# An FFT convolution with phase mixing: the inverse's pieces placed among the spectrum pieces, without idle matmuls

## The chip, the cores and the metric

The kernel runs on one core of one Trainium2 chip. The metric is the device time of one execution in microseconds. Before the change it was 2034.54 us, the median of three runs (2033.99 to 2038.23).

## What is computed

Two stages follow one another. The first convolves each of 8 sequences of 5696 tokens and 128 channels with one filter per channel, by a real FFT of twice the length. The second mixes tokens with two dense 5696 x 5696 matrices after a phase rotation, and ends with a small channel matmul.

```
L = 2 * S                                   # B, S, D = 8, 5696, 128
Yf = rfft(x, n=L, axis=1) * rfft(h, n=L, axis=0)[None]
x  = irfft(Yf, n=L, axis=1)[:, :S]
theta = x @ w_theta
y = w_tok_r @ (x * cos(theta)) + w_tok_i @ (x * sin(theta))
u = x + y
out = u + relu(u @ w_ch)
```

The change concerns only the first stage. In the profiled execution it takes the first 340 us or so, and the dense mixing most of the rest.

## The kernel before, in words

The FFT of length 11392 is split as 178 x 64 and done with matmuls against sine tables. The work is cut into eight groups, each two sequences (index `bp`) by half of the channels (`dh`, 64 channels). A group goes through four stages:

- A, `stage_a` (L251): 16 pieces of 4 matmuls (89 rows, 180 columns each). Each piece is copied from PSUM to the tile `a` by ScalarE (L258).
- B, `stage_b` with `f2` (L269): the spectrum in 12 pieces over the 90 frequencies of the first split, eight frequencies to a piece and two in the last, so 32 matmuls (64 rows, 64 columns) in each of eleven pieces and 8 in the last. ScalarE copies each to `xs` (L399, two buffers), and VectorE multiplies it twice with the filter's spectrum into `u_t` and `v_t` (L401).
- C, `stage_c` (L421, L422): 16 pieces of 16 matmuls (128 x 128). Every one reads all frequencies of `u_t` and `v_t`, so C can't begin before the last products of B. Each piece is scaled into the tile `g` (one buffer), mostly by VectorE (L429). ScalarE does some of the pieces with two instructions (L426, L427).
- D, `stage_d` (L444): the inverse in 7 pieces, six of 20 matmuls (90 rows, 89 columns) and one of 8. The first needs all of `g`. ScalarE copies each to `yt` (L447), and behind the last the result is stored to HBM on SP's queue.

All four stages draw their PSUM tiles from one ring of four buffers (`psum()`), in program order: a piece can't start before the piece four places earlier is copied out.

The loop over groups runs two stages of neighbouring groups together. Loop `g` first weaves C of group `g` with A of group `g + 1`, and then B of group `g + 1` with D of group `g`. The function `woven` gives every step of each list a place between two bounds and runs the steps in order of place, so that the order of each engine's work is the program's order here. With its bounds, C and A begin with three A pieces; B and D run as B0 D0 B1 B2 D1 B3 B4 D2 B5 B6 D3 B7 D4 B8 B9 D5 B10 B11 D6. The load of x for group `g + 2` is the last step of the list of A; its 16 DMAs are issued by GpSimd (L138). In the last loop there is no next group, and steps of the phase stage (`phase_step`, L728 and L515 to L551) are woven in instead.

Behind the last spectrum piece, `f2` issues 12 matmuls of 384 columns on tables (L275, `WARM`). They write columns of the piece's own PSUM tile that nobody reads.

Of the kernel before, what the change touches and what calls it, by code (L numbers as in the profile page):

```python
# [23 lines left out]
def kernel(  # L24
# [10 lines left out]
    nc = tc.nc  # L35
    B, S, D = x.shape
    assert D == 128
    P = 128
# [45 lines left out]
    CK = 8  # L84
    HD = D // 2
    EN = N2 // 2 + 1
    WARM = 12
    XP = HD + 4
    assert N1 * N2 == NF and NB * N2 == S and NB % 2 == 1 and K1 <= P
    CHK = [(c0, min(CK, K1 - c0)) for c0 in range(0, K1, CK)]  # L90
    NCK = len(CHK)
# [36 lines left out]
    groups = [(bp, dh) for dh in range(2) for bp in range(B // 2)]  # L128
# [45 lines left out]
    w_t2 = keep.tile([P, K1, 3 * N2], F16, tag="keep", name="w_t2")  # L174
# [83 lines left out]
                nc.scalar.activation(a_out, a_in, AF.Copy)  # L258
        return [lambda q=q: chunk(q) for q in range(0, HD, 4)], st

    def f2(a_st, c, warm=True):

        c0, ck = CHK[c]
        ps = psum()
        for j in range(ck):
            for ri in range(2):
                for e in range(2):
                    rows = slice(64 * e, 64 * e + 64)
                    nc.tensor.matmul(ps[:, e, j * HD:(j + 1) * HD],  # L269
                                     w_t2[rows, slot(e, c0 + j), N2 * (1 - ri):N2 * (3 - ri)],  # L270
                                     a_st["a"][rows, ri * K1 + c0 + j, :],
                                     start=(ri == 0), stop=(ri == 1))
        if c == NCK - 1 and warm:
            for n in range(WARM):
                nc.tensor.matmul(ps[:, n % 2, ck * HD:ck * HD + 384], w_t2[:, 2, :P],  # L275
                                 w_t2[:, 0:2, :].rearrange("p k n -> p (k n)"), start=True, stop=True)
        return ps[:, :, :ck * HD].rearrange("p e (k d) -> p e d k", k=ck)

    def woven(*lists):

        lists = [l if isinstance(l, tuple) else (l, 0.0, 1.0) for l in lists]
        steps = [(w0 + (i + 0.5) / len(l) * (w1 - w0), n, f)
                 for n, (l, w0, w1) in enumerate(lists) for i, f in enumerate(l)]
        for _, _, f in sorted(steps, key=lambda s: s[:2]):
            f()
# [8 lines left out]
    steps, a_h = stage_a(lambda q: h16[:NB].rearrange("p h n d -> p (h n) d")[:, :, q], (4, 6, 8, 10, 12, 14))  # L294
# [28 lines left out]

    def h_chunk(c):
        c0, ck = CHK[c]
        ps = f2(a_h, c, False)
        nc.scalar.activation(h_part(c)[:, 0], ps[:, 0], AF.Copy, scale=16.0 / NF)
        nc.vector.tensor_scalar(h_later[:, HD * c0:HD * (c0 + ck)].rearrange("p (d k) -> p d k", k=ck),
                                ps[:, 1], 16.0 / NF, None, op0=mult)
# [59 lines left out]
        nc.vector.tensor_scalar(sgn[:, :EN], sgn[:, :EN], half, None, op0=mult)  # L389
        nc.vector.tensor_scalar(sgn[:, EN:], sgn[:, EN:], odd, half, op0=mult, op1=mult)  # L390

    def stage_b(a_st, warm, refill):

        def chunk(c):
            c0, ck = CHK[c]
            hv = h_part(c)
            ps = f2(a_st, c, warm)
            xs = fs.tile([P, 2, HD, CK], F16, tag="xs", name="xs")
            nc.scalar.activation(xs[:, :, :, :ck], ps, AF.Copy)  # L399
            for r in range(2):  # L400
                nc.vector.tensor_tensor(  # L401
                    uv[r][:, :, :, c0:c0 + ck], xs[:, :, :, :ck],
                    hv[:, r:r + 1].to_broadcast([P, 2, HD, ck]), op=mult)
            if refill:
                src = hf_hbm[:, HD * c0:HD * (c0 + ck)]
                nc.sync.dma_start(h_flat(c)[:, :HD * ck], src)
                for p0 in (0, 64):
                    nc.sync.dma_start(h_flat(c)[p0:p0 + 64, HD * ck:], src[64 - p0:P - p0])
        return [lambda c=c: chunk(c) for c in range(NCK)]

    def stage_c(st, last):
        sg = sgn[:K1].unsqueeze(2).unsqueeze(1).to_broadcast([K1, 2, N2, 8])

        def chunk(q):
            if q == 0:
                st["g"] = fg.tile([P, 2 * N2, P], F16, tag="g", name="g_")
            ps = psum()
            for i in range(8):
                o = ps[:, i // 4, (i % 4) * P:(i % 4 + 1) * P]
                at = (q + i) * K1  # L420
                nc.tensor.matmul(o, u_t[:, at:at + P], r_u, start=True, stop=False)  # L421
                nc.tensor.matmul(o, v_t[:, at:at + P], r_v, start=False, stop=True)  # L422
            g_out = st["g"][:K1, :, q:q + 8].rearrange("p (r n) q -> p r n q", r=2)
            g_in = ps[:K1].rearrange("p a (q r n) -> p r n (a q)", q=4, r=2)
            if q % 16 == 0 and (last or q >= 64):
                nc.scalar.mul(g_out[:, :, :EN], g_in[:, :, :EN], sgn[:K1, 0:1])  # L426
                nc.scalar.mul(g_out[:, :, EN:], g_in[:, :, EN:], sgn[:K1, EN:EN + 1])  # L427
            else:
                nc.vector.tensor_tensor(g_out, g_in, sg, op=mult)  # L429
        return [lambda q=q: chunk(q) for q in range(0, 2 * HD, 8)]  # L430

    def stage_d(st, bp, dh, then=None):
        def chunk(n0, cn):
            if n0 == 0:
                st["yt"] = fy.tile([P, NB, N2], BF16, tag="yt", name="yt")
            g_, yt = st["g"], st["yt"]
            ps = psum()
            nq = 5 if cn == CN else cn
            for j in range(cn):
                n = n0 + j  # L440
                o = ps[:, j // nq, (j % nq) * NB:(j % nq + 1) * NB]
                for ri in range(2):
                    e_ = e_t[:K1, n, ri, :] if n < EN else e_t[:K1, N2 - n, ri, ::-1]
                    nc.tensor.matmul(o, g_[:K1, ri * N2 + n, :], e_, start=(ri == 0), stop=(ri == 1))  # L444
            y_out = yt[:, :, n0:n0 + cn].rearrange("p m (a q) -> p m a q", q=nq)
            y_in = ps[:, :cn // nq, :nq * NB].rearrange("p a (q m) -> p m a q", q=nq)
            nc.scalar.activation(y_out, y_in, AF.Copy)  # L447
            if n0 + cn == N2:
                if then is not None:
                    then(yt)  # L450
                for e in range(2):
                    t0 = H if then else 0
                    nc.sync.dma_start(
                        yt_hbm[dh * HD:(dh + 1) * HD, 2 * bp + e, t0:],
                        yt[64 * e:64 * e + 64].rearrange("p m n -> p (m n)")[:, t0:])
        return [lambda n0=n0, cn=cn: chunk(n0, cn) for n0, cn in CHN]
# [3 lines left out]
    def front(g, on_dve=()):  # L460
        if g >= len(groups):
            return [], []
        dh = groups[g][1]
        x16 = x16s[g].rearrange("p b n d -> p (b n) d")
        steps, a_st = stage_a(lambda q: x16[:NB, :, q], on_dve)
        return steps, stage_b(a_st, g > 0, dh == 0 and groups[g + 1][1] == 1)

    a0, b0 = front(0, (2, 4, 6, 8, 10, 12, 14))
    BATCH = ((0, 4), (4, 4), (8, 3), (11, 1))
# [11 lines left out]
    for n, f in enumerate(a0):  # L481
# [9 lines left out]
    e_left = [lambda f=f, n=n: f(*E_STEPS[n]) for f, n in (  # L491
        (e_table, 1), (e_index, 5), (e_table, 2), (e_index, 6), (e_table, 3),
        (e_table, 4), (e_table, 5), (e_table, 6))]
# [261 lines left out]
    for g, (bp, dh) in enumerate(groups):  # L755
        st = {}
        last = g + 1 == len(groups)
        if last:
            late_order.enter_context(tc.manual_schedule(engines={mybir.EngineType.Pool}))
        a_, b_ = front(g + 1, () if g else (5, 11))  # L760
        if last:
            for _ in range(3):
                steps0.pop(0)()
        now = [with_load(steps0.pop(0), n < 6) for n in range(9)] if last else []
        c_ = stage_c(st, last)
        if g + 2 < len(groups):
            a_ = a_ + [lambda g=g: load_x(g + 2)]
        woven((c_, 0.06 if a_ else 0.0, 1.0), (a_, 0.0, 0.55), now, ([] if g else e_left, 0.0, 0.9))
        if g == 0:
            in_order.close()  # L770
            first.close()
        if g + 2 == len(groups):
            xin.close()
            open_phases()
            load_ya0()
        now = [steps0.pop(0) for _ in range(3)] if last else []
        woven(b_, (stage_d(st, bp, dh, load_ya1 if last else None), 0.0, 1.1 if b_ else 1.0), now)
        if g + 2 == len(groups):
            load_ya1()
            open_ring()  # L780
            home_of[0] = tile_b(0, 0, None)
# [35 lines left out]
    bp = cp = wlp = ybp = None  # L817
# [258 lines left out]
    nxt, second, st = None, None, {}  # L1076
    ordered = ExitStack()
    for i, (k, p, tt, j0, s0, nj) in enumerate(stretches):
# [6 lines left out]
        if first_of_pair and tt == pairs[p][0]:  # L1085
            if p == 1:
                start_pass(p)
            else:
# [6 lines left out]
        woven = (tt is not None and end_of_pair and i + 1 < len(stretches)  # L1095
                 and stretches[i + 1][2] is not None)
# [36 lines left out]
        if tt is None:  # L1133
            if p:
                aside(True, False)
            if first_of_pair:
                q = M1 if p else M3
                ps = mps.tile([P, 512], F32, tag=f"m{q}", name=f"m{q}")
# [18 lines left out]
            if end_of_pair:  # L1157
# [5 lines left out]
                c, c0 = c_last  # L1163
# [161 lines left out]
```

## Time and profile before

| what | value |
|---|---|
| median of three runs | 2034.54 us |
| profiled execution | 2035.64 us, of which the span from first to last instruction is 2033.9 us |
| mean granted TensorE clock | 0.987 |
| busy: TensorE / VectorE / ScalarE / GpSimd | 1936.4 / 1573.3 / 655.1 / 964.0 us |
| first C of the loops of groups 1 to 6 | 109.92, 147.28, 186.33, 224.71, 261.95, 299.19 us |
| start of D's first piece after B's in the loop of group 5 | B0 at 280.72, D0 at 282.19 us |
| idle matmuls | 84, each 326 ns long; a block of 12 takes 1.96 us from its start to the next matmul |

In what follows, a line of a timeline gives start and length in us, the engine, the line of the kernel, the operation with output and input, and in brackets the idle time ahead of it and what ended that. A line of the table over stretches gives the stretch, its length, the busy time and number of instructions of TensorE's matmuls and weight loads, of VectorE, ScalarE and GpSimd, then the granted TensorE clock, the share of the DMA engines and the GB/s moved. The length of a matmul in a timeline is from its issue to its modelled end; matmuls overlap, so how long a series takes is read from starts.

### The profile page before, as it was taken

Reading aid. Unit: us, or ns where it says so; the run is one execution under the profiler, and the core shown is the slowest. Engines: PE = TensorE matmul, PEld = TensorE weight load, DVE = VectorE, ACT = ScalarE, POOL = GpSimd, SP = SyncE. Lnnn points to the kernel's source line nnn. Section 1 sums busy time; section 2 is a strip of 40 time slices with the busy share of each in tenths; the row PEclk is TensorE's granted clock in tenths of the full one; section 3 lists DMA queues with packets and bytes.
Section 4 is the critical chain, followed back from the end, with each engine's and each line's share of the span. In section 5 each row is a group of like instructions: output and inputs, shape, how many; then the busy total and the mean of one; then the engine's idle time right before and its main releaser. Section 6 shows DMA issues by size and latency. Waiting matters only on the chain.

```text
span 2033.9 us, 41286 instructions
## 1 busy us (share of the span) xinstructions
PE 1936.4 (95%) x15664; PEld 1073.2 (53%) x15841; DVE 1573.3 (77%) x2890; ACT 655.1 (32%) x1004; POOL 964.0 (47%) x1721
## 2 busy tenths in 40 slices
PE   6799999788999999999999999999999999999998
PEld 5688888654444444444444444444444444444444
DVE  8777778786788888888877669768677786777767
ACT  6788888851232323333210000011111111111111
POOL 8523322363364545455565554553545445354450
PEclk9799999998999999999999999999999999999999
DMA  9978975997898998989999899887878878788793
GB/s 115 64 84 124 89 87 165 266 272 139 163 174 177 174 178 154 180 170 181 171 168 164 121 241 243 131 149 129 152 135 146 149 129 144 137 146 147 133 157 85
DMA packets 487752, 312.05 MB, mean 153 GB/s; under 512 B 182887, under 2 KB 448615, under 8 KB 486567
## 3 DMA queue, kind: packets, MB, share of 16 engines
q0 software_dynamic: 321600, 155.29, 60.8%
q1 hardware_dynamic: 158784, 140.34, 24.0%
q10 hardware_dynamic: 7168, 13.76, 1.9%
q8 instruction: 124, 2.03, 0.4%
q14 instruction: 76, 0.62, 0.1%
HBM read 354.37 MB, written 90.29 MB: 219 GB/s over the span
## 4 chain that ended last, share of the span: by engine, by line
PE 66%; DMA 3%; DVE 3%; issue 1%; POOL 0%; ACT 0%; DVEq 0%; ACTq 0%
PE m L1262 62%; DMA b<-z_hbm 2%; DVE c L1269 1%; PE v L942 1%; PE utp L935 1%; PE m L1266 1%; PE m L1150 1%; DVE wt L855 1%; PE theta_ps L515 0%; PE tpz L883 0%; DMA yT<-yt_hbm 0%; PE m L1183 0%; POOL ring L631 0%; DMA ring<-in_moe_w_tok_r_dram 0%; DMA ring<-in_moe_w_tok_i_dram 0%
## 5 line engine op out<-in xcount | busy, mean ns | idle before, releaser
L631 POOL DMA_DIRECT2D ring<-in_moe_w_tok_i_dram x720 | 390.2, 552 | 652.8 <-DVE wt L855 554.0
L855 DVE STREAM_TRANSPOSE wt<-ring 128x384 f32<-128x384 f32 (+2 forms) x720 | 358.9, 523 | 115.1 <-PE m L1262 63.7
L631 POOL DMA_DIRECT2D ring<-in_moe_w_tok_r_dram x720 | 388.5, 553 | 124.8 <-DVE wt L855 79.5
L1262 PE MATMUL m<-b,wt 128*128 128x512 bf16 x1605 | 384.8, 379 | 4.1 <-DVE wt L855 2.1
L1262 PEld LDWEIGHTS <-wt 128*128 128x128 bf16 x1804 | 176.0, 98 | 216.4 <-DVE wt L855 5.1
L1269 DVE TENSOR_TENSOR c<-c,m 128x512 f32<-128x512 f32 x412 | 265.3, 669 | 0.4 <-PE m L1262 0.4
L937 ACT ACTIVATE ring<-utp 128x512 bf16<-128x512 bf16 x85 | 50.8, 597 | 575.8 <-PE utp L935 575.8
L138 POOL DMA_DIRECT2D x<-in_x_dram x128 | 99.6, 807 | 140.4 <-PE ps L251 132.8
L421 PE MATMUL ps<-r_u,u_t 128*128 128x128 f16 x1024 | 124.6, 220 | 6.9 <-DVE u_t L401 3.5
L1183 PE MATMUL m<-b,wt 128*128 128x512 bf16 x471 | 113.1, 387 | 12.0 <-DMA b<-zr_hbm 8.1
L422 PE MATMUL ps<-r_v,v_t 128*128 128x128 f16 x1024 | 123.6, 220 | 0.3
L932 ACT ACTIVATE ub<-c 128x512 bf16<-128x512 f32 x88 | 55.1, 628 | 185.8 <-DMA ring<-in_moe_w_tok_i_dram 103.8
L422 PEld LDWEIGHTS <-v_t 128*128 128x128 f16 x1024 | 100.6, 98 | 5.6 <-issue 4.2
L421 PEld LDWEIGHTS <-u_t 128*128 128x128 f16 x1024 | 100.6, 98 | 4.7 <-DVE u_t L401 4.7
L399 ACT ACTIVATE xs<-ps 128x1024 f16<-128x1024 f32 x96 | 91.5, 982 | 8.8 <-PE ps L269 2.6
L1183 PEld LDWEIGHTS <-wt 128*128 128x128 bf16 x528 | 51.5, 99 | 71.0 <-issue 17.1
L401 DVE TENSOR_TENSOR u_t<-xs,hs 128x1024 f16<-128x1024 f16 x96 | 64.2, 669 | 31.7 <-ACT xs L399 29.3
L885 ACT ACTIVATE ring<-tpz 128x512 bf16<-128x512 bf16 (+1 forms) x46 | 27.5, 597 | 148.8 <-PE tpz L883 123.7
L517 ACT ACTIVATE red<-theta_ps,magic 128x512 f32<-128x512 f32 (+1 forms) x46 | 31.6, 687 | 127.1 <-PE theta_ps L515 99.4
L269 PEld LDWEIGHTS <-w_t 64*128 64x128 f16 x3240 | 60.4, 102 | 22.0 <-issue 15.8
L401 DVE TENSOR_TENSOR v_t<-xs,hs 128x1024 f16<-128x1024 f16 x96 | 63.7, 664 | 0.0
L944 DVE SCALAR_TENSOR_TENSOR c<-v,c 128x512 f32<-128x512 f32 x88 | 59.9, 682 | 2.9 <-PE v L942 2.6
(2932 smaller groups left out, 3773.3 us busy)
## 6 DMA issues: line engine op xcount, KB each, us to landing
ring<-in_moe_w_tok_r_dram POOLq DMA_DIRECT2D x352, 96.0 KB, 4.6
ring<-in_moe_w_tok_i_dram POOLq DMA_DIRECT2D x352, 96.0 KB, 4.9
ring<-in_moe_w_tok_r_dram POOLq DMA_DIRECT2D x352, 80.0 KB, 4.4
ring<-in_moe_w_tok_i_dram POOLq DMA_DIRECT2D x352, 80.0 KB, 3.8
cp_hbm<-c SPq DMA_DIRECT2D x88, 256.0 KB, 2.3
c<-cp_hbm SPq DMA_DIRECT2D x88, 256.0 KB, 4.5
out_dram<-c SPq DMA_DIRECT2D x88, 256.0 KB, 4.2
yy<-y_hbm SPq DMA_DIRECT2D x84, 128.0 KB, 2.5
```

The lines of the kernel that those rows point to most:

```text
L138: nc.gpsimd.dma_start(x16[p0:p1, e, n0:n0 + 16, :HD], bass.AP(tensor=src.tensor, offset=src.offset + (p0 * N2 + n0) * D + dh * HD, ap=[[N2 ...
L269: nc.tensor.matmul(ps[:, e, j * HD:(j + 1) * HD], w_t2[rows, slot(e, c0 + j), N2 * (1 - ri):N2 * (3 - ri)], a_st["a"][rows, ri * K1 + c0 + ...
L399: nc.scalar.activation(xs[:, :, :, :ck], ps, AF.Copy)
L401: nc.vector.tensor_tensor(uv[r][:, :, :, c0:c0 + ck], xs[:, :, :, :ck], hv[:, r:r + 1].to_broadcast([P, 2, HD, ck]), op=mult)
L421: nc.tensor.matmul(o, u_t[:, at:at + P], r_u, start=True, stop=False)
L422: nc.tensor.matmul(o, v_t[:, at:at + P], r_v, start=False, stop=True)
L631: nc.gpsimd.dma_start(wb[32 * i:32 * i + 32, :ng, :nj * 64], bass.AP(tensor=a.tensor, offset=a.offset + row0 * S + p * H + i * QR + j0 * 6 ...
L855: nc.vector.transpose(wt.rearrange("p j t r -> p (j t r)").bitcast(F32).rearrange("p (j g t) -> p g j t", j=TJ, g=4)[:, :ng, :nj], wb[:, : ...
L944: nc.vector.scalar_tensor_tensor(c[:m], v[:m], 0.0, c[:m], op0=ALU.max, op1=ALU.add)
L1183: nc.tensor.matmul(ms[n // 2 * 2 + h], a[n][:, j, :, r], bts_of[p][jj][n % 2 * 2 + h][:, r, :], start=(n % 2 == 0 and jj == 0 and r == 0), ...
L1262: nc.tensor.matmul(ms[q], a[q][:, j, :, r], bts[jj][q][:, r, :], start=(jj == 0 and r == 0), stop=(jj == NJ - 1 and r == 1 and q not in left))
L1269: nc.vector.tensor_tensor(c, z, ms[q], op=op)
```

## The change

Four things are changed, all in the loop over groups:

1. B and D are no longer woven by places. A D piece follows every second B piece, five in all, and the last two D pieces come behind all of B: B0 B1 D0 B2 B3 D1 B4 B5 D2 B6 B7 D3 B8 B9 D4 B10 B11 D5 D6.
2. The 12 idle matmuls and all arguments for them go.
3. From the second loop on, the places of A end at 0.62 instead of 0.55, and C begins at 0 instead of 0.06. One A piece stands ahead of C instead of three, and A ends behind the ninth C piece instead of the eighth (the tenth in the loop of group 6, which has no load of x).
4. In all loops but the last, ScalarE takes three of the 16 pieces of `g` (q = 80, 96, 112) instead of four, and VectorE 13 instead of 12.

The order of the instructions on the queues of SP and GpSimd stays the same.

```diff
-    def f2(a_st, c, warm=True):
+    def f2(a_st, c):
...
-        if c == NCK - 1 and warm:
-            for n in range(WARM):
-                nc.tensor.matmul(ps[:, n % 2, ck * HD:ck * HD + 384], w_t2[:, 2, :P],
-                                 w_t2[:, 0:2, :].rearrange("p k n -> p (k n)"), start=True, stop=True)
...
-            if q % 16 == 0 and (last or q >= 64):
+            if q % 16 == 0 and (last or q >= 80):
...
-        return steps, stage_b(a_st, g > 0, dh == 0 and groups[g + 1][1] == 1)
+        return steps, stage_b(a_st, dh == 0 and groups[g + 1][1] == 1)
...
-        woven((c_, 0.06 if a_ else 0.0, 1.0), (a_, 0.0, 0.55), now, ([] if g else e_left, 0.0, 0.9))
+        woven((c_, 0.06 if a_ and not g else 0.0, 1.0), (a_, 0.0, 0.62 if g else 0.55), now,
+              ([] if g else e_left, 0.0, 0.9))
...
-        woven(b_, (stage_d(st, bp, dh, load_ya1 if last else None), 0.0, 1.1 if b_ else 1.0), now)
+        d_ = stage_d(st, bp, dh, load_ya1 if last else None)
+        if last:
+            woven(d_, now)
+        else:
+            for n, f in enumerate(b_):
+                f()
+                if n % 2 and n < NCK - 1:
+                    d_.pop(0)()
+            for f in d_:
+                f()
```

More of the change, by code (lines that the diff above doesn't have):

```diff
@@ L86 @@
     EN = N2 // 2 + 1
-    WARM = 12
     XP = HD + 4
@@ L325, in h_chunk @@
         c0, ck = CHK[c]
-        ps = f2(a_h, c, False)
+        ps = f2(a_h, c)
         nc.scalar.activation(h_part(c)[:, 0], ps[:, 0], AF.Copy, scale=16.0 / NF)
@@ L390, in s_table, with stage_b @@
         nc.vector.tensor_scalar(sgn[:, EN:], sgn[:, EN:], odd, half, op0=mult, op1=mult)
-    def stage_b(a_st, warm, refill):
+    def stage_b(a_st, refill):
         def chunk(c):
@@ L396, in chunk @@
             hv = h_part(c)
-            ps = f2(a_st, c, warm)
+            ps = f2(a_st, c)
             xs = fs.tile([P, 2, HD, CK], F16, tag="xs", name="xs")
```

## The prediction

> **What bounds the kernel now.** I read the page first (busy time, slices), then the timelines of ScalarE and TensorE over one loop over a group, then tables of busy time over stretches of 3.41 us, because the granted clock changes only on a grid of that length. Names: A is `stage_a` (L251), B a spectrum piece (L269), W the idle matmuls (L275), C `stage_c` (L421, L422), D a piece of the inverse (L444). The part that changes is the first 340 us; everything behind it is TensorE work that begins when it ends.
>
> ```profile
> PE 1936.4 (95%) x15664; PEld 1073.2 (53%) x15841; DVE 1573.3 (77%) x2890; ACT 655.1 (32%) x1004; POOL 964.0 (47%) x1721
> ...
> PEclk9799999998999999999999999999999999999999
> ```
>
> TensorE's 95% is a mean that hides the groups. In the loop of group 5 the first C starts at 261.95, B from 280.72, the next first C at 299.19: 37.24 us. In C and A TensorE has no gap, it is the limit. In B and D it is ScalarE; its row of operations:
>
> ```profile
> 281.46 1.02 ACT L399 ACTIVATE xs<-ps 128x1024 f16<-128x1024 f32 x1 [0.26 <-ACT g__6324 L427]
> 283.29 0.92 ACT L447 ACTIVATE yt<-ps 128x890 bf16<-128x890 f32 x1 [0.81 <-PE ps L444]
> 284.10 1.93 ACT L399 ACTIVATE xs<-ps 128x1024 f16<-128x1024 f32 x2
> 285.90 0.93 ACT L447 ACTIVATE yt<-ps 128x890 bf16<-128x890 f32 x1
> ...
> 295.62 0.97 ACT L447 ACTIVATE yt<-ps 128x890 bf16<-128x890 f32 x1
> 296.41 1.53 ACT L399 ACTIVATE xs<-ps 128x1024 f16<-128x1024 f32 x2
> 297.82 0.44 ACT L447 ACTIVATE yt<-ps 128x356 bf16<-128x356 f32 x1
> ```
>
> See that copies follow each other without gaps, except 0.81 us for the first D. From starts: an `xs` copy takes 0.90 us (the last, two columns instead of eight, 0.47), a `yt` copy 0.80. Twelve `xs` and six `yt` end at 297.82; then TensorE:
>
> ```profile
> 294.13 1.08 PE L269 MATMUL ps<-a__6305,w_t 64*128 64x64 f16 x40
> 295.14 2.12 PE L275 MATMUL ps<-w_t 128*128 128x384 f16 x12
> 297.10 0.49 PE L444 MATMUL ps<-e_t,g__6324 90*128 90x89 f16 x8
> 297.43 1.12 PE L251 MATMUL ps<-f_t,x 89*128 89x180 f16 x12
> 299.19 0.23 PE L421 MATMUL ps<-r_u,u_t 128*128 128x128 f16 x1 [0.64 <-DVE u_t L401]
> ```
>
> C waits for the last products on VectorE, 1.37 us behind the last `xs`. W, the last D and three A cover that wait but for 0.64 us. Last, stretches of the clock's grid:
>
> ```profile
> 39.55:42.97 3.42, 2.36 (x25) 1.99 (x23) 3.39 (x6) 2.83 (x5) 3.03 (x6) 1.00 0.39 81
> 94.16:97.58 3.42, 1.68 (x76) 1.40 (x72) 2.89 (x6) 3.39 (x5) 0.19 (x1) 1.00 1.43 91
> 97.58:100.99 3.41, 3.37 (x84) 3.15 (x85) 2.20 (x4) 2.41 (x3) 0.00 (x0) 0.50 0.03 6
> 135.12:138.54 3.42, 2.42 (x96) 2.09 (x96) 3.03 (x6) 3.41 (x5) 0.00 (x0) 1.00 0.71 44
> ...
> 213.63:217.04 3.41, 3.41 (x96) 3.19 (x88) 3.27 (x6) 3.40 (x5) 0.00 (x0) 0.50 0.85 53
> ...
> 363.82:367.23 3.41, 1.78 (x27) 1.42 (x24) 3.41 (x6) 3.37 (x7) 1.59 (x5) 1.00 1.20 281
> ```
>
> The first figure behind the length is TensorE's busy time, the third from the end its clock. A thin stretch (94.16) is followed by one at half clock. Busy time alone does not sort them (363.82 has 1.78 us and no drop; 39.55 has 2.36 and is followed by half clock). Columns by the share of the 128 rows do, at 0.434 ns a column (C: 128 columns each 55.6 ns). Drops follow stretches with 1.22 us of it (64 B, 12 D at 94.16), 1.32 (176.08), 1.21 (210.22) and 1.36 (25 A at 39.55); none follows 1.63 (135.12) or 1.67 (363.82).
>
> **The change, part by part.**
>
> *Order of B and D* (loops 0 to 6). Now B0 B1 D0 B2 B3 D1 ... B8 B9 D4 B10 B11 D5 D6. Before the last `xs` ScalarE copies five `yt` instead of six: 0.80 us. D0 waits for the last g copy (VectorE, 280.83 to 282.05); ScalarE has a second `xs` to do meanwhile, so of its 0.81 us about 0.1 stays: 0.7. The products come 1.37 us behind the last `xs` as before. Together -1.5 us a loop, 7 loops: **-10.5**. The `yt` copies put off go into C, where ScalarE has 0.45 us gaps between A copies. SP's and POOL's instructions keep their order; SP's store of `yt` leaves some 1 us later against C, and the next write of `yt` is 18 us away.
>
> *A spread over 0.62 instead of 0.55, C from 0* (loops 1 to 6, which have an A and `g` above 0). One A piece stands before C instead of three; two more fall into the TensorE-bound part, 0.32 us each: 6 x 0.64 = **+3.8**. The x load of the group after starts behind the last A, so 1.5 us later against C; the last loads landed at 288.4 by DMA traffic and the next A starts at 297.43, so 9 us of slack become 6: nothing.
>
> *W away* (7 x 12). 1.96 us of TensorE each, beside the wait for VectorE, so worth nothing in a smooth loop. But W writes into B11's buffer, and ScalarE's last `xs` waited for it 1.14 us at 183.13 and 0.30 at 221.94: **-1.4**. It is also what keeps the stretch before C busy; that is costed below.
>
> *One g copy from ScalarE to VectorE* (seven groups). ScalarE loses 1.24 us, VectorE gains 1.14. In loops 1 to 6 both have gaps at that place (VectorE 0.31 us behind each copy, ScalarE 0.45): nothing. In loop 0 ScalarE is full from 84.30 to 92.02 with tables and g copies, and the first `xs` follows; gain between 0 and 1.24, I take **-1.0**, since TensorE waits there (1.17 us for ScalarE's g copy).
>
> Without the clock: -10.5 + 3.8 - 1.4 - 1.0 = **-9.1 us**.
>
> *The clock at the start of C* (loops 1 to 6; in loop 7 the phase steps fill TensorE). Take the first C as 0. The last `xs` ends at -1.37; backwards by 0.47, 0.90, 0.80, 0.90: B10's copy starts -2.74, D4's -3.54, B9's -4.44. There are four PSUM buffers, so D5 starts when B9 is copied (-3.4), D6 follows, A0 when B10 is copied (-1.7). B11 ended at -4.3: in 4.3 us TensorE has D5 0.95, D6 0.34 and A0 0.32 us, in the weighted measure 0.54 + 0.22 + 0.22 = 0.98 us. A stretch that starts between -4.7 and -2.4 has at most the 1.36 us that still drop the clock; one between -5.2 and -1.9 at most the 1.63 that do not. So 67 to 97% of all positions on the grid drop; I take 0.8. The half-clock stretch then begins 3.41 us later and lies 1.6 to 3.4 us inside C, where TensorE is the limit: loss 0.8 to 1.7, mean 1.35 us. 6 x 0.8 x 1.35 = **+6.5**. Where it begins before C, TensorE is partly idle in it and may stay slow for another 1.7 us; full stretches are released after one (213.63 to 217.04), emptier ones not (half clock from 459.39 to 469.63). Possible for a third of the drops, 2.4 us; I take half: **+1.2**. Bounds per transition are 0 (no drop) and 3.4 (two full stretches).
>
> [...]
>
> *The drops of before* (97.58, 179.50, 213.63) follow gaps of 1.6 to 1.8 us charged to "issue", while x loads run. They fall between D pieces, which stay. The loads now reach about 0.9 us deeper into B. Bounds -1.5 and +3, I take 0.
>
> Sum: -9.1 + 6.5 + 1.2 = -1.4 us. The profiled execution took 2035.64 (span 2033.9, 1.7 around it), so 2034.2 for it; it lies 1.1 above the median of 2034.54, from which the same step gives **2033.1 us**.
>
> **Rivals.**
> 1. *Only a gap about as long as a whole stretch halves the clock, so it does not drop here, or rarely.* For it: the threshold is read from seven stretches, and the longest half-clock spans (459.39, and around 60) do hold long gaps. Against it: four drops at more weighted work than 0.98 us. [...] Time: 2034.5 - 9.1 = 2025.4; faster by over 0.2% once the loss is below (9.1 - 4.1) / 6 = 0.83 us a transition.
> 2. *Slower: the half clock lasts two stretches at each transition.* For it: 459.39 to 469.63 held it three. Against: three drops in B and D ended after one. 1.35 + 1.7 = 3.05 us each, 18.3 in all: +9.2, 2043.7. It decides from (9.1 + 4.1) / 6 = 2.2 us a transition.
>
> **How the numbers follow.** 0.2% is 4.1 us, about what a measurement of this kernel tells from no change (the three runs lie 4.2 apart). Gain and loss cancelling (2030.5 to 2038.6): 0.44. Rival 1: 0.32. Rival 2: 0.24. These are the chances of same, faster and slower. The likeliest alone gives 2033.1, 2030.5 to 2037. The range reaches into both rivals, 2026 to 2041, leaving about 0.1 at either end.
>
> **What would show it.** In the timeline, first C to first C near 36.3 us where the clock holds and 37.3 to 39 where it drops; `xs` two by two with five `yt` before the last; a wait of about 1.3 us for `u_t` before C; stretches at 0.50 clock at the starts of C, most of six. No such stretches: rival 1. Pairs of them: rival 2. A wait of A for x, or longer gaps under "issue", would make the sum wrong in a way that I priced at nothing.

## The result, and the profile after

The changed kernel takes 2042.12 us (median of 14 runs, 2038.78 to 2050.03), the kernel before beside it 2035.47 us (14 runs): the ratio is 1.0037 with a 95% interval of 1.0024 to 1.0049. By the ratio it is slower by about 7.5 us, not faster by 1.4. The median lies 1.1 us above the range that was given. The profiled execution took 2041.76 us with a span of 2040.0 us.

TensorE has less to do and is slower. The first lines are the busy times and the granted clock on the page of the changed kernel:

```profile
PE 1930.0 (95%) x15580; PEld 1073.8 (53%) x15757; DVE 1582.2 (78%) x2897; ACT 647.2 (32%) x990; POOL 960.6 (47%) x1721
...
PEclk9888999899999999999999999999999999999999
```

The 84 idle matmuls are gone from the count. Of the first ten slices of the clock (51 us each), four now read 8; before, one read 7 and one 8. Times the span, the missing clock gives a figure that every run has: (1 - mean granted clock) x span. I call it lost clock; the time that the kernel loses by it is less wherever TensorE would have waited anyway. It is 39.1 us in the mean of the 14 runs, against 26.0 us over 30 runs of the kernel before made beside the first experiments: +13.1 us.

The order on ScalarE is what was forecast. Its timeline in the loop of group 5:

```profile
282.43 1.94 ACT L394 ACTIVATE xs<-ps 128x1024 f16<-128x1024 f32 x2 [0.26 <-ACT g__6247 L422]
284.25 0.93 ACT L442 ACTIVATE yt<-ps 128x890 bf16<-128x890 f32 x1
...
296.04 1.34 ACT L394 ACTIVATE xs<-ps 128x1024 f16<-128x1024 f32 x2
297.25 1.25 ACT L442 ACTIVATE yt<-ps 128x890 bf16<-128x890 f32 x2
```

The 0.81 us of idle time at the first D piece is gone, and two `yt` copies follow the last `xs`. In this loop the clock holds, and it takes 36.32 us from first C (262.43) to first C (298.75), as forecast (36.3); before it took 37.24. The trouble is in other loops: those of groups 0 to 6 take 42.39, 39.39, 39.19, 38.08, 36.78, 36.32 and 42.02 us, and took 43.42, 37.36, 39.05, 38.38, 37.24, 37.24 and 39.10.

Two things are larger. The first is the wait ahead of C. TensorE's timeline and, below it, stretches of the clock's grid:

```profile
260.80 0.47 PE L250 MATMUL ps<-f_t,x 89*128 89x180 f16 x4 [0.43 <-ACT xs L394]
262.43 0.23 PE L416 MATMUL ps<-r_u,u_t 128*128 128x128 f16 x1 [1.17 <-DVE u_t L396]
```

```profile
104.29:107.71 3.42, 2.20 (x58) 2.01 (x50) 3.03 (x6) 3.42 (x6) 0.00 (x0) 1.00 0.02 5
107.71:111.12 3.41, 2.24 (x21) 2.09 (x20) 1.52 (x4) 1.81 (x4) 0.00 (x0) 0.50 0.51 107
111.12:114.53 3.41, 3.41 (x31) 3.41 (x30) 1.93 (x2) 1.54 (x3) 0.00 (x0) 0.50 0.85 197
...
295.44:298.85 3.41, 1.82 (x34) 1.66 (x34) 3.16 (x7) 3.41 (x6) 0.00 (x0) 1.00 0.02 5
298.85:302.27 3.42, 3.42 (x33) 3.34 (x33) 1.37 (x2) 1.09 (x2) 0.00 (x0) 0.50 0.79 163
```

Where C began at 108.99 and at 298.75, the stretch ahead is thin, and the next is at half clock (0.50): two stretches at the first, one at the second. The stage from first C to first B takes 21.77 and 20.80 us there, against 19.26 where the clock holds. At the C of 187.57 half clock that began in B at 179.39 runs 2.1 us into C (20.14 us); at the other three C's of these loops the clock holds.

The second is the time under "issue". TensorE's waits over the loops of groups 1 to 6, before (110 to 335 us; "issue" stands where the view found nothing that TensorE waited for):

```profile
PE ps L269 <- issue: 7.3, 9, 1.8
PE ps L421 <- DVE u_t L401: 2.6, 5, 0.7
PE ps L444 <- issue: 2.4, 2, 1.6
```

and after (109 to 337 us; B is L268 now, C L416, D L439):

```profile
PE ps L268 <- issue: 10.5, 7, 3.5
PE ps L439 <- issue: 7.2, 13, 1.5
PE ps L416 <- DVE u_t L396: 5.8, 5, 1.2
```

Columns: time in total, number, longest. Of the 17.7 us after, 1.9 are six waits of 0.32 us ahead of D0, where TensorE waited 0.8 us for the last g copy before. That leaves 15.8 against 9.7 us. The longest gap, 3.5 us among the B matmuls between 176.68 and 182.17, stands around the start of half clock from 179.39 to 189.63.

What TensorE waits for there can be found among the DMA transfers. Queue 8, of the kind "instruction", makes 123 transfers of 16 KB in the changed kernel, one for every 256 instructions of TensorE in the trace (31,481). The gaps over 0.36 us end behind such transfers:

| kernel | transfer on queue 8 | gap on TensorE | from the transfer's end to the gap's end |
|---|---|---|---|
| before | 95.20 to 96.09 | 95.84 to 97.62 | 1.53 us |
| changed | 137.61 to 138.59 | 138.38 to 140.06 | 1.47 us |
| changed | 178.14 to 179.82 | 177.73 to 181.25 | 1.43 us |
| changed | 286.96 to 287.93 | 287.88 to 289.36 | 1.43 us |

From 66 to 345 us there are 10 such gaps in the kernel before and 13 in the changed one. All end 1.25 to 1.68 us behind the end of a transfer, and at each of them TensorE has begun 449 to 451 instructions more than 256 for every transfer finished before that one. The 14 traces of this document have 133 of them, with the same counts and 1.2 to 1.9 us. I read that as TensorE having run out of instructions, and waiting for the next 256.

At the end of the span the difference is 6.1 us in these two executions: 2.5 by the first phase step (337.47 against 334.98), and the rest in later stages, which the change does not touch and whose own half-clock stretches fall elsewhere. From the first C of group 7 to the end the 14 traces take between 1693.2 and 1699.9 us. So the total of one execution does not tell the kernels apart; the medians do, and a trace is best read for the loops alone.

### The profile page after: what moved, and what is told of

Its sections match the earlier page's. It is cut to its first block, busy times and chain, and to the rows that moved or that the text cites. A ratio compares the mean times of both kernels' runs of the same rounds, so it can differ in the third digit from the quotient of the medians.

```text
span 2040.0 us, 41110 instructions
## 1 busy us (share of the span) xinstructions
PE 1930.0 (95%) x15580; PEld 1073.8 (53%) x15757; DVE 1582.2 (78%) x2897; ACT 647.2 (32%) x990; POOL 960.6 (47%) x1721
## 4 chain that ended last, share of the span: by engine, by line
PE 63%; DVE 5%; DMA 3%; issue 2%; POOL 1%; ACT 0%; DVEq 0%; SPq 0%; POOLq 0%
PE m L1267 58%; DVE c L1274 2%; DMA ring<-in_moe_w_tok_i_dram 1%; POOL ring L626 1%; PE utp L940 1%; PE v L947 1%; DVE wt L860 1%; PE m L1271 1%; PE m L1155 1%; DMA b<-z_hbm 1%; PE theta_ps L510 0%; PE tpz L888 0%; DMA c<-cp_hbm 0%; DMA ring<-in_moe_w_tok_r_dram 0%; DMA cp_hbm<-c 0%
## 5 line engine op out<-in xcount | busy, mean ns | idle before, releaser
L416 PE MATMUL ps<-r_u,u_t 128*128 128x128 f16 x1024 | 129.0, 224 | 10.3 <-DVE u_t L396 5.8
L417 PE MATMUL ps<-r_v,v_t 128*128 128x128 f16 x1024 | 128.0, 223 | 0.0
L416 PEld LDWEIGHTS <-u_t 128*128 128x128 f16 x1024 | 102.6, 100 | 7.0 <-DVE u_t L396 6.9
L396 DVE TENSOR_TENSOR u_t<-xs,hs 128x1024 f16<-128x1024 f16 x96 | 64.1, 668 | 25.8 <-ACT xs L394 23.5
L268 PEld LDWEIGHTS <-w_t 64*128 64x128 f16 x3240 | 59.9, 102 | 26.1 <-issue 21.1
L250 PE MATMUL ps<-f_t,x 89*128 89x180 f16 x512 | 58.0, 253 | 7.2 <-ACT xs L394 5.2
```

What stands on the lines that cost most here:

```text
L250: nc.tensor.matmul(ps[:, i // 2, (i % 2) * 2 * K1:(i % 2 + 1) * 2 * K1], lhs(q + i), f1_t[:NB], start=True, stop=True)
L268: nc.tensor.matmul(ps[:, e, j * HD:(j + 1) * HD], w_t2[rows, slot(e, c0 + j), N2 * (1 - ri):N2 * (3 - ri)], a_st["a"][rows, ri * K1 + c0 + ...
L396: nc.vector.tensor_tensor(uv[r][:, :, :, c0:c0 + ck], xs[:, :, :, :ck], hv[:, r:r + 1].to_broadcast([P, 2, HD, ck]), op=mult)
```

## The experiments

Theory 1 is the prediction's step: the thin stretch ahead of C drops the clock, and C pays. Theory 2 is the rival that formed on reading the trace: gaps under "issue" inside B and D grew while x loads run, and the half clock follows those. Each kernel was timed beside the kernel before.

### Idle matmuls: back in the new kernel, out of the old

The first (e1) puts W back behind B11 of the changed kernel:

```diff
-    def f2(a_st, c):
+    def f2(a_st, c, warm=True):
...
+        if c == NCK - 1 and warm:
+            for n in range(WARM):
+                nc.tensor.matmul(ps[:, n % 2, ck * HD:ck * HD + 384], w_t2[:, 2, :P],
+                                 w_t2[:, 0:2, :].rearrange("p k n -> p (k n)"), start=True, stop=True)
...
```

> The changed kernel with the 12 idle matmuls put back behind B11 (ahead of D5 and D6). Theory 1 (the half clock that begins in the thin stretch ahead of C takes the gain): the stretches ahead of C hold 2 us more of matmuls, so no half clock begins at C; the time falls below the kernel before, by 4 to 8 us. Theory 2 (the gaps under 'issue' in B, while x loads run, grew, and the half clock follows them): the gaps and the half clock inside B and D stay, and the time stays 2 to 7 us above before, apart from at most 2 us.

Measured: 2038.81 us, ratio 1.0007 (0.9997 to 1.0018), lost clock 29.2 us. Nothing else but 84 matmuls that compute nothing recovers about 6 of the 7.5 us. No half clock begins at a C; the time is not below before, though, so this is theory 1 for most of the loss and not for all.

The second (e2) takes W out of the kernel before:

```diff
-    WARM = 12
+    WARM = 0
```

> The kernel before with no idle matmuls and nothing else. Theory 1: D6 and three A pieces alone are left in the 4 us ahead of C, the clock halves at most of six transitions, 4 to 8 us slower than before. Theory 2: the idle matmuls hide nothing that limits, and only delay B11's copy when B is late: 0 to 2 us faster than before.

Measured: 2044.04 us against 2036.72, ratio 1.0034 (1.0022 to 1.0047), lost clock 37.3 us. That is theory 1's forecast of the time, and about the effect of the change by size. Its forecast of the place is borne out in part: in the one profiled execution half clock stands at two of the six C's (107.18 and 301.74), not at most of them, and two more spans begin inside B and D (141.31 and 212.99, the second three stretches long). The stretches at one C, which began at 302.03, are:

```profile
298.25:301.66 3.41, 1.86 (x20) 1.54 (x19) 3.27 (x7) 3.40 (x7) 0.00 (x0) 1.00 0.02 5
301.66:305.08 3.42, 3.05 (x28) 3.00 (x29) 1.45 (x4) 1.96 (x4) 0.00 (x0) 0.51 1.04 210
```

### The weave of A: old in the new kernel, new in the old

The changed kernel with A and C woven as before (e3):

```diff
-        woven((c_, 0.06 if a_ and not g else 0.0, 1.0), (a_, 0.0, 0.62 if g else 0.55), now,
-              ([] if g else e_left, 0.0, 0.9))
+        woven((c_, 0.06 if a_ else 0.0, 1.0), (a_, 0.0, 0.55), now, ([] if g else e_left, 0.0, 0.9))
```

> The changed kernel with A and C woven as before (three A pieces ahead of C, A ends 1.5 us earlier, so the x loads leave 1.5 us earlier). Theory 1: 0.4 us more work ahead of C and 3.8 us less in C; 3 to 6 us faster than the changed kernel, half clock at C in fewer loops. Theory 2: the gaps under 'issue' shrink to about those of before (some 11 us in all against 17), 5 to 9 us faster than the changed kernel, so a little faster than before.

Measured: 2032.87 us against 2036.72, ratio 0.9982 (0.9973 to 0.9992): faster than before, and by 0.55% faster than the changed kernel, some 11 us. That is more than either theory had. The timeline of its TensorE shows why:

```profile
256.76 1.31 PE L439 MATMUL ps<-e_t,g__5288 90*128 90x89 f16 x28
258.35 0.89 PE L250 MATMUL ps<-f_t,x 89*128 89x180 f16 x8 [0.28 <-ACT xs L394]
259.55 0.47 PE L250 MATMUL ps<-f_t,x 89*128 89x180 f16 x4 [0.31 <-ACT yt L442]
260.01 0.23 PE L416 MATMUL ps<-r_u,u_t 128*128 128x128 f16 x1
```

Three A pieces fill the wait, and C starts without one. Undisturbed loops take 35.77 us, 0.55 less than those of the changed kernel. Lost clock is 30.1 us, and half clock stands at one C of six (108.81).

The same change of weave alone, made in the kernel before (W, order and share as they were):

```diff
-        woven((c_, 0.06 if a_ else 0.0, 1.0), (a_, 0.0, 0.55), now, ([] if g else e_left, 0.0, 0.9))
+        woven((c_, 0.06 if a_ and not g else 0.0, 1.0), (a_, 0.0, 0.62 if g else 0.55), now,
+              ([] if g else e_left, 0.0, 0.9))
```

> The kernel before with the new weave of A and C alone (one A piece ahead of C, A to 0.62). Theory 1 (thin stretch ahead of C): the idle matmuls still fill it, so only the two A pieces moved into C cost, 6 x 0.64 = 3.8 us slower than before, with hardly more half clock. Theory 2 (x loads that start 1.5 us later run deeper into B and make the gaps under 'issue' longer): more, 6 to 10 us slower, with the sum of those gaps up from 11.5 us.

Measured: 2041.71 us against 2035.83, ratio 1.0029 (1.0016 to 1.0043), 5.9 us. Undisturbed loops take 37.73 us, 0.49 more than before, so six of them explain 2.9 us; lost clock is 30.6 us against 26.6, and the gaps under "issue" rose from 11.5 to 13.5 us in the profiled execution, one of them 4.06 us. Theory 1's price for the two A pieces (0.64 a loop) is about right. Whether the rest is theory 2's stays open: the interval, 3.3 to 8.8 us, holds both forecasts, and the profiled execution is one of the fastest of the 12.

### The order of B and D alone

The kernel before with the new loop over B and D, and nothing else (e4):

```diff
-        woven(b_, (stage_d(st, bp, dh, load_ya1 if last else None), 0.0, 1.1 if b_ else 1.0), now)
+        d_ = stage_d(st, bp, dh, load_ya1 if last else None)
...
+            for n, f in enumerate(b_):
+                f()
+                if n % 2 and n < NCK - 1:
+                    d_.pop(0)()
...
```

> The kernel before with the new order of B and D alone (idle matmuls, weave of A and share of g as before). Theory 1: the gain of the order without the clock's loss, 6 to 10 us faster than before. Theory 2: if the order itself makes the gaps under 'issue' larger, no gain: within 3 us of before or slower.

Measured: 2037.17 us against 2036.72, ratio 0.9999 (0.9990 to 1.0008). The best loops are 36.55 us, 0.7 shorter than before and not 1.5, and lost clock is 30.0 against 26.0. W now stands ahead of two D pieces, and in five loops ScalarE's last `xs` waits for it, 4.3 us in all against 1.4 before. The gaps under "issue" add to 14.3 us (0.32 us waits ahead of D0 left out) against 11.5, both in the loops of groups 0 to 6. So theory 1's 6 to 10 us fall. With A woven as before, the order gains only with W gone (e9 below). With the new weave of A it gains with W too: e1 and e5 differ by the order and by the share of `g`, and their ratios are 1.0007 and 1.0029.

### Filling only the wait for u_t

The changed kernel with 8 idle matmuls at the head of the first C piece in the loops of groups 1 to 6 (e6):

```diff
             ps = psum()
+            for n in range(fill if q == 0 else 0):
+                nc.tensor.matmul(ps[:, n % 2, :384], w_t2[:, 2, :P],
+                                 w_t2[:, 0:2, :].rearrange("p k n -> p (k n)"), start=True, stop=True)
...
-        c_ = stage_c(st, last)
+        c_ = stage_c(st, last, 8 if g and not last else 0)
```

> The changed kernel with 8 idle matmuls in the buffer of the first C piece, right ahead of it, so that they fill the wait for u_t and delay no copy of B11. Theory 1: half clock at the starts of C goes; 5 to 9 us faster than the changed kernel, about as the kernel before or a little faster. Theory 2: the half clock comes from gaps in B and stays: at most 3 us faster than the changed kernel.

Measured: 2038.40 us against 2035.83, ratio 1.0013 (1.0001 to 1.0025); lost clock 32.8 us. It gains about 5 us by ratio (1.0037 to 1.0013), the low end of theory 1. No half clock begins within 0.5 us of a C, but seven stretches between 106 and 331 us are left, all inside B and D.

### Without the loads of x

Both kernels without the loads for groups 2 to 7 (e7 from the changed kernel, e8 from the one before):

```diff
-            a_ = a_ + [lambda g=g: load_x(g + 2)]
+            x16s[g + 2] = x16s[g + 1]
```

> The changed kernel that loads x for the first two groups only and uses the second's x for all that follow (the loads of groups 2 to 7 are left out, so those groups convolve another group's x). Theory 2: the gaps under 'issue' in B vanish but for the short waits ahead of D0; 7 to 13 us faster than the changed kernel, more than what the same does to the kernel before. Theory 1: the half clock at C stays; at most 4 us faster.

Measured: 2038.90 us against 2035.83, ratio 1.0010 (0.9997 to 1.0022), lost clock 37.2 us.

> The kernel before with the same loads of x left out (groups 2 to 7 convolve the second group's x). Theory 2: the gaps under 'issue' (11.5 us in six loops) vanish, 3 to 7 us faster than before, and none of the three half-clock stretches inside B and D is left. Theory 1 says nothing else here; if the gaps stay, x loads do not make them.

Measured: 2033.76 us, ratio 0.9988 (0.9978 to 0.9998), lost clock 23.5 us. The gaps inside B and D are gone in the loops of groups 1 to 5 of both (0.32 us ahead of D0 apart), so nearly all of them come from having x loads in flight. In e11 below, which has no such loads either, two of over 0.36 us are left there (1.34 us at 208.45 and 0.45 at 211.91), and e7 and e8 keep some in the loop of group 6, e8 one in that of group 0. With the loads, 9 to 16 of some 32 instruction transfers between 109 and 300 us begin when TensorE has, by the count of 450, fewer than 150 instructions left (12 in the kernel before, 11 in the changed one); in e7, e8 and e11 it is 2, 3 and 5. A transfer itself takes 1.07 us in the mean with the loads (1.07 before, 1.04 in the changed kernel) and 1.06 without. So with the loads the next instructions begin to arrive late, but do not arrive more slowly.

The old kernel gains 2.4 us by leaving the loads out, the changed one 5.5. Both gain less than theory 2 said. The difference, 3.1 us, would be the share of the 7.5 that comes by way of the loads; but by the intervals of the three ratios it is uncertain by some 4 us either way. The time of B and D in the traces speaks for it, as the table in the part on the prediction shows.

The changed kernel without loads shows theory 1 with almost nothing beside it. Two transitions by stretches; the other four look the same:

```profile
143.10:146.51 3.41, 1.76 (x32) 1.54 (x31) 3.27 (x7) 3.40 (x6) 0.00 (x0) 1.00 0.01 2
146.51:149.93 3.42, 3.14 (x29) 3.09 (x30) 1.44 (x3) 1.43 (x3) 0.00 (x0) 0.51 0.77 160
180.66:184.07 3.41, 1.77 (x32) 1.54 (x31) 3.26 (x7) 3.41 (x7) 0.00 (x0) 1.00 0.51 135
184.07:187.48 3.41, 3.17 (x29) 3.12 (x30) 1.44 (x3) 1.42 (x3) 0.00 (x0) 0.50 0.51 136
```

The 32 matmuls of the thin stretch are D5, D6 and one A piece (28 + 4), 0.98 us in the weighted measure. At all six transitions the half clock begins 0.2 to 0.3 us ahead of C. C and A take 20.67 us against 19.26: 1.41 us lost at each, 8.5 in six. B and D take 16.86, and the loops 37.48 to 37.55 us. Without loads the old kernel's loops take 37.23, with no half clock between 72 and 365 us.

The kernel of e3 with the same edit (e11):

> The kernel of e3 with the loads of x of groups 2 to 7 left out (those groups convolve the second group's x). If three A pieces ahead of C lift the stretch there above what drops the clock, loops of 35.8 us with no half clock at all, and 5 to 8 us faster than before; if not, half clock at every C as in e7 and loops locked to 37.5 us, slower than e8.

Measured: 2030.61 us against 2036.00, ratio 0.9973 (0.9961 to 0.9984), lost clock 31.7 us. The time fits the first case, the trace does not: half clock stands at four of the six transitions (from 111.5, 145.6, 258.2 and 292.4), and one loop of five is 35.75 us, the others 36.97 to 37.20. Three A pieces raise the stretch, but not always enough; this is one execution, and slower than the median of its runs.

### The share of g

The kernel of e3 with ScalarE's fourth piece back:

```diff
-            if q % 16 == 0 and (last or q >= 80):
+            if q % 16 == 0 and (last or q >= 64):
```

> The kernel of e3 (new order, no idle matmuls, A woven as before) with ScalarE taking four pieces of g as before, so that it differs from e4 only by the idle matmuls and from e3 only by the share. If the share gains only in the first loop, 0 to 2 us slower than e3, still faster than before; the idle matmuls of e4 then cost 2 to 4 us in the new order. If the share carries e3's gain, it ends within 1 us of before.

Measured: 2030.06 us against 2036.00, ratio 0.9975 (0.9964 to 0.9985). It is the fastest of all by median, 5 us below before. Against e4, from which it differs by W alone, it shows what W costs in the new order with three A pieces ahead of C: 0.24% by the ratios, some 5 us.

And the share alone in the kernel before:

```diff
-            if q % 16 == 0 and (last or q >= 64):
+            if q % 16 == 0 and (last or q >= 80):
```

> The kernel before with the share of g alone changed (ScalarE 3 pieces, VectorE 13). By the prediction: ScalarE is relieved in the loop of group 0, 1.0 us faster. By the trace of the changed kernel: there VectorE's extra copy stands ahead of the table steps that ScalarE's sines wait for, so the first xs of that loop comes about 1 us later, 1 to 2 us slower; the other loops do not change.

Measured: 2038.36 against 2037.51 us, ratio 1.0002 (0.9993 to 1.0011): neither forecast is told from zero. But the gain of 1 us in the first loop is not there. ScalarE in that trace:

```profile
86.71 0.67 ACT L169 ACTIVATE e_t<-e_all,zero_b 90x445 f16<-90x445 f32 x1 [1.99 <-DVE e_all L163]
```

The same sine in the kernel before waits for nothing:

```profile
85.44 0.66 ACT L169 ACTIVATE e_t<-e_all,zero_b 90x445 f16<-90x445 f32 x1
```

VectorE's extra copy stands in its queue ahead of the table step that this sine waits for, and the first `xs` starts at 93.19 instead of 91.91. The other traces agree: from first C to first B the loop of group 0 takes 24.4 to 25.4 us in the eight kernels with the new share, and 23.0 to 24.0 in the six with the old one. B and D win part of it back, and the whole loop takes 43.3 us against 42.4 in the mean. So the new share costs about 0.9 us there. By their times, whether e9 beats e3 by the share stays open; their intervals overlap.

### One D piece more behind B

The kernel of e3 with four D pieces among B and three behind:

```diff
-                if n % 2 and n < NCK - 1:
+                if n % 2 and n < NCK - 3:
```

> The kernel of e3 with four D pieces among the B pieces and three behind B11. ScalarE has one yt copy less ahead of the last xs (0.8 us a loop), but the first C's buffer then comes free only behind three yt copies, about 0.6 us later than the last products. Within 1 us of e3, or up to 3 us faster if the fuller stretch ahead of C keeps the clock up more often; slower if the buffer decides.

Measured: 2039.22 us, ratio 1.0017 (1.0005 to 1.0029), slower than e3 by 0.35%. B and D take 17.59 us at best, 16.89 in e3. TensorE ahead of a C shows that the buffer decides:

```profile
301.95 0.47 PE L250 MATMUL ps<-f_t,x 89*128 89x180 f16 x4 [0.33 <-ACT yt L442]
302.31 0.26 PE L416 MATMUL ps<-r_u,u_t 128*128 128x128 f16 x1
```

The last A piece ahead of C waits for the third `yt` copy, and C follows it. Half clock begins within 0.2 us of the start of C at three transitions and runs into C at a fourth; lost clock is 34.1 us.

## Why the prediction was wrong, point by point

- **Order of B and D**, -1.5 us a loop. Right where nothing disturbs: from first B to first C 17.06 us in the loop of group 5, 18.47 before, -1.4. With W kept the same order gains 0.7 at best (e4).
- **Two A pieces into C**, +0.64 a loop. 19.26 against 18.77 from first C to first B, +0.5. The step was worked out for C alone. The two pieces also left the stretch ahead of C, and there they are worth more: with them C does not wait for `u_t` at all (e3), and the change from one to three A pieces is worth 11 us in the new order without W.
- **W away**. What it does to the smooth loop was right: nothing. In the kernel before its removal costs 7 us (e2); in the new order it costs about 6 us with one A piece ahead of C (e1) and gains 5 with three (e9 against e4).
- **The clock at the start of C**, +6.5 and +1.2. In e7 it comes out as worked out: the stretch of 0.98 us ahead of C is in its trace to the digit, and the loss in C is 1.41 us where 1.35 was taken; six of six drop, so 8.5 us where both terms together had 7.7. In the changed kernel as it ran, with loads, only three of the six C's lose (2.5, 0.9 and 1.5 us). Two follow the thin stretch ahead of C (at 107.71, where half clock lasts two stretches, and 298.85); the third has its half clock from a gap in B, at 179.39. So the size came out smaller in that execution, about 5 us. The half clock at 141.84 also begins in B and D and ends 3.1 us ahead of C.
- **The drops of before**, taken at 0 with bounds -1.5 and +3. This is the step that failed, with the next one: what B and D lose while x loads run was taken not to grow. The x loads were seen to reach deeper into B, and priced at nothing. Gaps went from 9.7 to 15.8 us, and B and D became shorter by 6.6 us instead of 11.9 in the profiled executions; without loads they became shorter by 10.8. By the medians, leaving the loads out gains 5.5 us after and 2.4 before, so +3.1 us, uncertain by some 4.
- **The delay of B11's copy by W**, -1.4. It exists only where gaps make B late: in e8 it is gone but for 0.26 us in the loop of group 6. It was no gain of its own.
- **The share of g**, -1.0. The step overlooked what is queued behind the added copy on VectorE. From first C to first B the loop of group 0 became 1.1 us longer; the time of e12 alone, +0.4 us with an interval of -1.4 to +2.2, does not tell it from zero.

The traces give the account by stages. One profiled execution each, from the first C of group 0 to that of group 7, in us:

| part | forecast | without loads, e7 less e8 | with loads, changed less before |
|---|---|---|---|
| B and D, loops of groups 0 to 6 (order, W's delay, drops of before) | -11.9; without W's delay -10.5 | -10.8 | -6.6 |
| C and A, loops of groups 1 to 6 (A pieces and clock) | +11.5 | +11.4 | +7.9 |
| C and A, loop of group 0 (share of `g`) | -1.0 | +1.2 | +1.1 |
| together | -1.4 | +1.8 | +2.4 |

Without loads the two large terms come out as they were worked out, and only the share fails. With loads B and D miss by 5.3 us, and the clock at C, by losing less than forecast, hides 3.6 of it. The loads cost B and D 7.6 us in the changed kernel (against e7), 3.5 in the kernel before (against e8) and 4.2 in e3 (against e11). So most of the growth goes with the new weave of A, which lets the loads leave later; that rests on single executions.

By the medians e7 is slower than e8 by 0.22%, 4.5 us (1 to 8 by the two intervals), and the change with loads by 7.5. What these have beyond the 1.8 and 2.4 us of the loops was not seen in a trace: the profiled execution of e7 (lost clock 30.5 us) is milder than the mean of its runs (37.2), and that of the changed kernel, 6.1 us slower than the one before, lost 3.6 of it behind the first C of group 7.

Rival 2 ended on the right side, by luck: its mechanism, two stretches of half clock at every transition, shows at one of the two drops at C in the changed kernel, and at none of six in e7, and it did not name the loads. Rival 1 fell: the stretch at 143.10 in e7, with waits of 0.43 and 1.17 us ahead of the C at 146.79, holds 32 matmuls and is followed by half clock, and in the changed kernel waits of 0.63 and 0.42 us in the stretch at 104.29 were enough. What shows at every drop is the length of a stretch: all half-clock spans of the first 340 us, before and after, are multiples of 3.41 us.

## What to carry to other kernels

A wait can cost more than itself. In e7 1.17 us of it ahead of C went with 1.41 us lost in C, because the thin stretch of 3.41 us that held most of it was followed by half clock. So where a trace shows the granted clock going with the work in such a stretch, add up the work in every position of it before dropping filler matmuls, and price what the half clock then slows. Real work moved into the wait was the better filler here: three A pieces behind two D pieces gain 5 us (e9), with W besides 0 (e4), and with one A piece and no W the kernel loses 7.5. When a load moves by a microsecond, look at what else runs worse while it is in flight, the engine's own instructions included (gaps of 15.8 us against 9.7), and when a copy changes engine, at what stands behind it (a wait of 1.99 us in e12).

## What the runs showed of the hardware

The weighted measure told drops from no drops in these traces. It is columns x rows/128 x 0.434 ns (a C matmul, 128 columns on 128 rows, took 55.6 ns at full clock), summed over the matmuls that start in each stretch of the grid. In the traces of the kernel before and of the changed one, from 72 to 345 us, eight stretches at full clock were followed by half clock, and hold 0.89 to 1.25 us of it in 3.41; 138 were not, and hold 1.33 us or more. In the traces of all 14 kernels it was 50, none with more than 1.32 us, and 1003, none with less than 1.29. The longest gap in a stretch does not sort them: in the changed kernel it was 0.63 us in the stretch from 104.29, which was followed by half clock, and 1.58 us in the one from 87.23, which was not. The measure also went with the end of half clock: of 12 half-clock stretches in the two traces, four were followed by another and hold at most 1.32 us, eight by full clock and hold at least 1.40. Of 67 in all 14, none with more than 1.36 us was followed by another, and none with less than 1.26 by full clock. These are counts over this kernel's variants; what sets the clock was not tried. The prediction's gap between 1.36 and 1.63 was read from six stretches, with matmuls counted that only end in them; with 1.3, an estimate from the counts above, the positions that drop go from about -4.7 to -2.4, two thirds of the grid.

In e7 the half clock locked the loops to the grid. A loop without drops would take 16.86 + 19.26 = 36.12 us there. It takes 37.48 to 37.55, and eleven times 3.413 is 37.54, so that each transition falls on the same place of the grid as the one before (stretches from 143.10 and 180.66) and drops again. This explains six of six, though the chance of 0.8 alone would give that too in one case of four. With loads the changed kernel's loops of groups 1 to 6 take 36.32 to 42.02 us, and nothing locks.

TensorE stopped, as I read the counts, for want of instructions. In the changed kernel they came in 123 transfers of 16 KB for 31,481 instructions, 256 to a transfer; at 133 gaps in 14 traces (23 of them in the traces of before and after) TensorE stopped 449 to 451 instructions past the multiple of 256 that had arrived, and went on 1.2 to 1.9 us behind the end of the next transfer. Leaving out loads of x into another buffer took away most of these gaps: by the view of TensorE's waits over the loops of groups 1 to 6, "issue" goes from 9.7 to 1.8 us in the kernel before (e8), and in the changed one, the 1.9 us of waits ahead of D0 apart, from 15.8 to 2.0 (e7). The longest gap was 1.8 us before and 3.5 in the changed kernel. The transfers then begin earlier: 2 and 3 of some 32 late ones in e7 and e8, 9 to 16 with the loads. By which path the loads delay their beginning was not tried.
